# Attention with pooled queries and two MLPs: maxima tiles of every other query, and row maxima read back from memory with half the transfers

## The chip, the cores and the metric

The kernel runs on one core of one Trainium2 chip. The metric is the device time of one execution in microseconds (us), lower is better. In the trace the engines are PE (TensorE's matmuls), PEld (TensorE's weight loads, which overlap PE), DVE (VectorE), ACT (ScalarE), POOL (GpSimd) and SP (SyncE, which issues nearly all DMAs; SPq is its queue of instructions).

## What is computed

Queries are averaged in pairs, attention runs over 2 x 8 heads with 576 pooled queries and 1152 keys of width 64, and the result, as 1152 tokens of width 512, goes through two MLPs (mish, then ELU) of inner width 2048:

```python
q_pool = q.reshape(B, H, S // 2, 2, D).mean(axis=3)      # (2, 8, 576, 64)
scores = scale * np.matmul(q_pool, k.transpose(0, 1, 3, 2))
scores = scores - np.max(scores, axis=-1, keepdims=True)
attn = np.exp(scores)
attn = attn / (np.sum(attn, axis=-1, keepdims=True) + 1e-09)
x = np.matmul(attn, v)             # heads side by side: (1152, 512)
h = x @ w_in;  x = (h * np.tanh(softplus(h))) @ w_out    # first MLP
h = x @ w_in2; x = np.where(h > 0, h, np.exp(h) - 1) @ w_out2
```

## The kernel before

**Pairs of heads.** Attention works on 8 pairs of heads one after the other, head 0 on partitions 0 to 63 and head 1 on partitions 64 to 127. A pair takes 18 steps: 9 blocks of 128 keys (kt) for the first 256 queries (c = 0), then 9 for the other 320 (c = 1). In a step `qk` (L363) forms the transposed scores, keys on partitions and queries along the free axis, as a sum of four matmuls a head: three products of high and low parts of K and Q, and a fourth that adds a row, the negated maximum of each query's scores, with a matrix `unit` that copies row 0 (head 0) or row 64 (head 1) of the tile `tops` to all 128 keys. ACT then takes the exponent (L372). `av` (L443) multiplies with V.

**The maxima.** The row must be known before a pair's scores are exponentiated, so it is made while the pair before is worked on. `peak_mm` multiplies the high parts again, now with queries as weights, so that 128 queries lie on partitions and keys along the free axis: tiles 0 to 3 of 128 queries (L279 for the first 1024 keys, L286 for the last 128 keys of all four tiles), and the last 64 queries of both heads together (L293). DVE takes maxima of them (`peak`, L300, L302, L304) and `top` writes them, negated, to `neg`: one partition a query, one column a tile and head. So they lie down a column and must become a row. That is done through memory: `top_out` (L336) writes `neg` to `hopm` in DRAM, `top_in` (L342, L347) reads it back along the free axis of `tops`. Each pair from 1 on does this twice: a **first round** for tiles 0 and 1, whose row is needed at the pair's first step by the fourth matmuls (128x256), and a **second round** for tiles 2 and 3 and the last 64 queries, needed nine steps later (128x320). Pair 0 uses no memory for it: `flip` turns its maxima with matmuls, and ACT copies them to `tops` (L326).

**Order of the work.** Everything is in program order on each engine, written out by a table: `PREP` and `PLAN` give for each item the step at which its instructions are put on their queue (`top` is the step of `top_out` after the last maximum, and that of `top_in` after it). SP issues its DMAs strictly in that order, so that an issue that waits or takes long holds up those behind it: behind the first round's reads stand the sums' write (`sum_out`, L415) and the next pair's K (`load_k`, L226), ahead of them a part of the MLP weights (L109) and of V (L239). ACT's copy of the high part of K (`high_k`, L256) waits for that load in ACT's own order, with exponents behind it. After the pairs come the two MLPs, `h_mm` (L178) and `out_mm` (L736).

Of the kernel before, what the change touches and what calls it, by code (L numbers as in the profile page):

```python
# [11 lines left out]
F32 = mybir.dt.float32  # L12
F32R = mybir.dt.float32r
# [3 lines left out]
ALU = mybir.AluOpType  # L17
AX = mybir.AxisListType
# [4 lines left out]
def tile_pool_attention_mish_elu_mlp(  # L23
# [16 lines left out]
    nc = tc.nc  # L40
    B, H, S, D = v.shape
    NT, DM = out.shape
    DFF = moe_w_in.shape[1]
    P = 128
# [3 lines left out]
    NQ = SQ // P  # L48
# [18 lines left out]
    dp = ctx.enter_context(tc.tile_pool(name="hop", bufs=2, space=bass.MemoryType.DRAM))  # L67
# [115 lines left out]
    def attention():  # L183
        with ExitStack() as st:
            ap = st.enter_context(tc.tile_pool(name="attn", bufs=2))
# [3 lines left out]
            def take():  # L189
                i = 2 * next(ring)  # L190
                return banks[:, i:i + 2]

            half = [slice(0, D), slice(D, P)]
# [4 lines left out]
            def fixed(name, shape, dt, one=()):  # L198
                x = ap.tile(shape, dt, name=name, bufs=1)
                y = x.bitcast(F32) if dt is F32R else x  # L200
                nc.gpsimd.memset(y, 0.0)
                for r in one:
                    nc.gpsimd.memset(y[r:r + 1], 1.0)
                return x

            tops = [fixed(f"top{i}", [P, SQ], F32R) for i in range(2)]
            blks = [fixed(f"blk{i}", [P, P], F32R) for i in range(2)]
            unit = fixed("unit", [P, P], F32R, one=(0, D))
            pad = fixed("pad", [P, NQ + 1, 2, D], F32)
# [5 lines left out]
            raw_k, raw_q, kh, kl, qh, ql, vs = {}, {}, {}, {}, {}, {}, {}  # L215
            hops, tots, rbs, stat, neg, pts, adds, sc, sums_, acc, xs = {}, {}, {}, {}, {}, {}, {}, {}, {}, {}, {}
# [50 lines left out]
            def evs(n):  # L267
                return EVW if n else EVN

            def peak_mm(n, e):  # L270
                t, j = evs(n)[e]
                kw = 512 if n else KB
                if e == 0:
                    stat[n] = ap.tile([P, NQ + 1, 2, 3], F32, tag="stat", name="stat")
                    neg[n] = ap.tile([P, NQ + 1, 2], F32R, tag="neg", name="neg")
                pt = sc[n, e] = take()
                if t < NQ:
                    for h in range(2):
                        nc.tensor.matmul(  # L279
                            pt[:, h, :kw], qh[n][half[h], t * P:(t + 1) * P], kh[n][half[h], j * kw:(j + 1) * kw],  # L280
                            start=True, stop=True,
                        )
                elif t > NQ:
                    for x in range(NQ):
                        for h in range(2):
                            nc.tensor.matmul(  # L286
                                pt[:, h, x * P:(x + 1) * P], qh[n][half[h], x * P:(x + 1) * P], kh[n][half[h], S - P:],
                                start=True, stop=True,
                            )
                else:  # L290
                    side = banks[:, 6, 512 - P:]
                    for i, x in enumerate((pt[:, 0], pt[:, 1], side)):
                        nc.tensor.matmul(x, blks[n % 2], kh[n][:, 512 * i:min(512 * (i + 1), S)], start=True, stop=True)  # L293

            def peak(n, e):
                t, j = evs(n)[e]
                kw = 512 if n else KB
                pt, m = sc.pop((n, e)), stat[n]
                if t < NQ:
                    nc.vector.tensor_reduce(m[:, t, :, j], pt[:, :, :kw], axis=AX.X, op=ALU.max)  # L300
                elif t > NQ:
                    nc.vector.tensor_reduce(m[:, :NQ, :, 2].rearrange("p t h -> p h t"), pt.rearrange("p h (t k) -> p h t k", k=P), axis=AX.X, op=ALU.max)  # L302
                else:
                    nc.vector.tensor_reduce(m[:, t, 0, 0:2], pt, axis=AX.X, op=ALU.max)  # L304
                    nc.vector.tensor_reduce(m[:, t, 0, 2:3], banks[:, 6, 512 - P:], axis=AX.X, op=ALU.max)
                if e == (4 if n else 5):
                    top(n, 0, 2)
                elif e == len(evs(n)) - 1:
                    top(n, 2, NQ)

            def top(n, t0, t1):
                m, g = stat[n], neg[n] if n else pad[:, :, :, 0]
                nc.vector.tensor_reduce(g[:, t0:t1, :], m[:, t0:t1], axis=AX.X, op=ALU.max, negate=True)
                if t1 == NQ:
                    nc.vector.tensor_reduce(g[:, t1, 0:1], m[:, t1, 0:1], axis=AX.X, op=ALU.max, negate=True)


            def flip(t0, t1):
                pt = take()[:, 0]
                for t in range(t0, t1):  # L320
                    nc.tensor.matmul(
                        pt[:, (t - t0) * P:(t - t0 + 1) * P], pad[:, t].rearrange("p h r -> p (h r)"), ident,
                        start=True, stop=True,
                    )
                if t0 < NQ:
                    nc.scalar.copy(tops[0][:, t0 * P:t1 * P], pt[:, :(t1 - t0) * P])  # L326
                else:
                    for h in range(2):
                        nc.scalar.copy(tops[0][half[h], NQ * P:], pt[half[h], half[h]])

            def top_out(n, t0, t1):
                if t0 == 0:
                    hops[n] = dp.tile([P, NQ + 1, 2], F32, tag="hopm", name="hopm")
                e = slice(2 * t0, 2 * t1 + (t1 == NQ))
                hop, g = (x.rearrange("p t h -> p (t h)")[:, e] for x in (hops[n], neg[n]))
                nc.sync.dma_start(out=hop, in_=g.bitcast(F32))  # L336

            def top_in(n, t0, t1):
                hop, row = hops[n], tops[n % 2]
                for h in range(2):  # L340
                    r = h * D
                    nc.sync.dma_start(  # L342
                        out=row[r:r + 1, t0 * P:t1 * P].rearrange("o (t p) -> o t p", p=P).bitcast(F32),
                        in_=hop[:, t0:t1, h].rearrange("p t -> t p").unsqueeze(0),
                    )
                    if t1 == NQ:
                        nc.sync.dma_start(  # L347
                            out=row[r:r + 1, NQ * P:].bitcast(F32), in_=hop[half[h], NQ, 0:1].rearrange("p o -> o p")
                        )

# [174 lines left out]
            for n in range(n_pairs):  # L527
                s0 = n * NS
                if n:
                    prep = PREP[min(n, 2)]  # L530
                    for i in range(2):
                        at(s0 + prep["load_q"][i], "sp", load_q, n, slice(0, SQ), slice(i, i + 1))
                        at(s0 + prep["load_k"][i], "sp", load_k, n, kcut[i])
                        at(s0 + prep["load_v"][i], "sp", load_v, n, i)
                        at(s0 + prep["high_k"][i], "act", high_k, n, kcut[i])
                        at(s0 + prep["low_k"][i], *(("rest", low_k, n, nc.vector) if i == 0 else ("pool", low_k, n, nc.gpsimd)), kcut[i])
                    at(s0 + prep["pool_q"], "pool", pool_q, n, nc.gpsimd)
                    at(s0 + prep["high_q"], "act", high_q, n)
                    at(s0 + prep["blk_q"], "act", blk_q, n)
                    at(s0 + prep["low_q"], "pool", low_q, n, nc.gpsimd)  # L540
                    for e, r in enumerate(prep["peak"]):
                        at(s0 + r // 2, ("peak", "late")[r % 2], peak_mm, n, e)
                        at(s0 + r // 2, "dve", peak, n, e)
                    for (i, o), r, t0, t1 in zip(prep["top"], (prep["peak"][4], prep["peak"][-1]), (0, 2), (2, NQ)):
                        at(s0 + r // 2 + i, "sp", top_out, n, t0, t1)
                        at(s0 + r // 2 + i + o, "sp", top_in, n, t0, t1)
                plan = LAST if n == n_pairs - 1 else PLAN
                for c in range(2):
# [5 lines left out]
                    t0 = s0 + plan["total"][c]  # L554
# [39 lines left out]
            for e in (0, 3, 1, 4, 2, 5):  # L594
                peak_mm(0, e)
                peak(0, e)
            spots = [banks[:, 6:8]]
            qk(0, 0, 0, 1, spots[0], slice(3))
            for e in range(6, 8):
                peak_mm(0, e)  # L600
            flip(0, 2)
            for e in range(6, 8):
                peak(0, e)
# [15 lines left out]
            s = 0  # L619
            while s < last + 9:  # L620
                n, c, kt = s // NS, (s % NS) // KT, s % KT
# [5 lines left out]
                m = 2 if not c and kt in two else 0 if not c and kt - 1 in two or s < 1 else 1  # L627
# [215 lines left out]
    with tc.manual_schedule():  # L843
        attention()
        mlps()
# [36 lines left out]
```

## Time and profile before

| | |
|---|---|
| time, median of 3 runs | 634.15 us (634.05 to 636.31) |
| time of the profiled execution | 635.57 us |
| its span, first to last instruction | 633.8 us |
| PE busy | 616.9 us (97%) |
| DVE, ACT, POOL busy | 445.9, 335.1, 197.9 us (70%, 53%, 31%) |
| DMA packets | 50797, of which 17656 under 512 B |

The span is 1.8 us less than the time of the same execution. Attention takes about the first 228 us of it, the MLPs the rest. PE is the busiest engine by far, so time is to be had where it stands still, or where its own work gets shorter or longer.

### The profile page before, as it was taken

What the parts mean: (1) busy time and instruction counts of PE and PEld (TensorE: products, weight loads), DVE (VectorE), ACT (ScalarE), POOL (GpSimd) and SP (SyncE); (2) the same over time, 40 slices, a digit from 0 to 9 for tenths busy, and PEclk for the clock granted to TensorE, in tenths of its full rate; (3) what the DMA queues carried; (4) which work ended last, traced back from release to release, by engine and by line L of the source; (5) the groups of instructions that cost most, each with busy time, mean ns of one, the idle gap of its engine ahead of it and who ended that gap; (6) DMA issues with size and microseconds to landing.
All of it is one profiled execution on the core that took longest, in us unless ns stands there. A gap on an engine that the chain in (4) does not pass through costs nothing.

```text
span 633.8 us, 11509 instructions
## 1 busy us (share of the span) xinstructions
PE 616.9 (97%) x4498; PEld 535.2 (84%) x4498; DVE 445.9 (70%) x705; ACT 335.1 (53%) x675; POOL 197.9 (31%) x191
## 2 busy tenths in 40 slices
PE   5899999999999999999999999999999999999997
PEld 3667676676776689999999999999999999999995
DVE  5868767787787468647548657759878788995453
ACT  3665546555565544434344553456666657664441
POOL 5666565657653511101104323333210101100000
PEclk9999999999999999999999999999999999999999
DMA  4234252442523425223232222222232223300111
GB/s 140 84 99 123 67 134 60 131 111 66 132 64 89 89 76 176 67 67 104 68 97 82 85 71 97 97 70 62 72 99 68 66 68 100 109 25 11 40 51 50
DMA packets 50797, 53.34 MB, mean 84 GB/s; under 512 B 17656, under 2 KB 40248, under 8 KB 50744
## 3 DMA queue, kind: packets, MB, share of 16 engines
q1 hardware_dynamic: 50520, 52.29, 28.6%
q8 instruction: 35, 0.57, 0.4%
q10 hardware_dynamic: 224, 0.33, 0.2%
q14 instruction: 18, 0.15, 0.1%
HBM read 50.14 MB, written 2.47 MB: 83 GB/s over the span
## 4 chain that ended last, share of the span: by engine, by line
PE 86%; DMA 6%; DVE 3%; SPq 2%; issue 1%; ACT 1%; DVEq 0%; ACTq 0%
PE banks L178 32%; PE banks L736 31%; PE banks L363 10%; PE banks L443 8%; DMA top<-hopm 3%; PE banks L279 2%; PE banks L398 2%; DVE stat L300 1%; DMA hopm<-neg 1%; PE banks L293 1%; DVE stat L302 1%; DMA kr<-in_k_dram 1%; SPq L342 1%; DMA raw<-in_moe_w_in_dram 1%; DMA qr<-in_q_dram 1%
## 5 line engine op out<-in xcount | busy, mean ns | idle before, releaser
L178 PE MATMUL banks<-XH,wh 128*128 128x384 f32 x384 | 129.5, 337 | 0.0
L178 PE MATMUL banks<-XL,wh 128*128 128x384 f32 x384 | 129.4, 337 | 0.0
L178 PE MATMUL banks<-XH,wl 128*128 128x384 f32 x384 | 129.4, 337 | 0.0
L123 POOL TENSOR_SCALAR wf<-wf 128x512 f32<-128x512 f32 x64 | 43.6, 682 | 256.2 <-ACT wf L119 225.8
L372 ACT ACTIVATE pt<-banks 128x640 f32<-128x640 f32 (+2 forms) x136 | 88.0, 681 | 63.1 <-PE banks L363 62.7
L300 DVE TENSOR_REDUCE stat<-banks 128x2 f32<-128x1024 f32 (+1 forms) x68 | 77.9, 1171 | 13.2 <-PE banks L279 13.0
L443 PE MATMUL banks<-pt,vr 128*64 128x320 f32 (+1 forms) x576 | 79.6, 414 | 0.0
L178 PEld LDWEIGHTS banks<-XH,wh 128*128 128x128 f32 x384 | 72.0, 188 | 2.3 <-issue 0.5
L178 PEld LDWEIGHTS banks<-XL,wh 128*128 128x128 f32 x384 | 72.0, 188 | 1.8
L178 PEld LDWEIGHTS banks<-XH,wl 128*128 128x128 f32 x384 | 72.0, 188 | 0.0
L690 ACT ACTIVATE gh<-banks 128x384 fp32r<-128x384 f32 x48 | 23.7, 493 | 78.7 <-PE banks L178 78.7
L736 PE MATMUL banks<-gh,wl 128*128 128x384 f32 x192 | 64.5, 336 | 0.0
L736 PE MATMUL banks<-gl,wh 128*128 128x384 f32 x192 | 64.5, 336 | 0.0
L736 PE MATMUL banks<-gh,wh 128*128 128x384 f32 x192 | 64.4, 335 | 0.0
L443 PEld LDWEIGHTS banks<-pt,vr 128*64 128x64 f32 x576 | 37.9, 136 | 27.9 <-issue 5.5
L383 POOL TENSOR_TENSOR add<-pt 128x640 f32<-128x640 f32 (+1 forms) x30 | 43.0, 1434 | 52.4 <-ACT pt L372 52.3
L736 PE MATMUL banks<-wh,gl 128*128 128x512 f32 x144 | 56.2, 390 | 0.0
L736 PE MATMUL banks<-wl,gh 128*128 128x512 f32 x144 | 56.2, 390 | 0.0
L736 PE MATMUL banks<-wh,gh 128*128 128x512 f32 x144 | 56.2, 390 | 0.0
L693 DVE TENSOR_TENSOR gl<-g,gh 128x384 fp32r<-128x384 f32 x48 | 31.1, 649 | 34.1 <-ACT g L691 34.1
L383 POOL TENSOR_TENSOR add<-add,pt 128x640 f32<-128x640 f32 (+1 forms) x31 | 47.1, 1521 | 17.9 <-DVE add L383 11.7
L363 PE MATMUL banks<-QH,KH 64*128 64x320 f32 (+1 forms) x288 | 49.8, 332 | 1.2 <-DVE stat L300 0.6
(85 smaller groups left out, 1220.9 us busy)
## 6 DMA issues: line engine op xcount, KB each, us to landing
raw<-in_moe_w_in_dram SPq DMA_DIRECT2D x28, 512.0 KB
raw<-in_moe_w_out_dram SPq DMA_DIRECT2D x28, 512.0 KB
vr<-in_v_dram SPq DMA_DIRECT2D x16, 288.0 KB
qr<-in_q_dram SPq DMA_DIRECT2D x14, 288.0 KB
kr<-in_k_dram SPq DMA_DIRECT2D x7, 384.0 KB
raw<-in_moe_w_in_dram SPq DMA_DIRECT2D x8, 256.0 KB
raw<-in_moe_w_out_dram SPq DMA_DIRECT2D x8, 256.0 KB
out_dram<-part SPq DMA_DIRECT2D x8, 256.0 KB
```

What stands on the lines that cost most here:

```text
L123: nc.gpsimd.tensor_scalar(self.f, self.f, HUGE, -HUGE, op0=ALU.min, op1=ALU.max)
L178: nc.tensor.matmul(pt[:, :TB], w[:, kk * P:(kk + 1) * P], x[:, kk, tk], start=(i == 0), stop=(i == len(terms) - 1))
L279: nc.tensor.matmul(pt[:, h, :kw], qh[n][half[h], t * P:(t + 1) * P], kh[n][half[h], j * kw:(j + 1) * kw], start=True, stop=True,)
L300: nc.vector.tensor_reduce(m[:, t, :, j], pt[:, :, :kw], axis=AX.X, op=ALU.max)
L363: nc.tensor.matmul(pt[:, h, t * w:(t + 1) * w], x[half[h], k0:k0 + P] if x is not None else unit[half[h], :], y[half[h], cols], start=(i = ...
L372: nc.scalar.activation(pts[n, c][:, kt:kt + m], sc.pop((n, c, kt)), AF.Exp, scale=SCALE)
L383: eng.tensor_tensor(d, d if i is None else p[:, i], p[:, j], op=ALU.add)
L398: nc.tensor.matmul(pt[32 * g:32 * (g + 1), :w], ones[:, :32], x[:, h, z * w:(z + 1) * w], start=(i == 0), stop=(i == len(srcs) - 1), tile_ ...
L443: nc.tensor.matmul(acc[n, c][half[h], :w], vs[n][:, h, kt, :], pts[n, c][:, kt, h, :], start=(kt == 0), stop=(kt == KT - 1),)
L690: nc.scalar.activation(gh, h, AF.Mish)
L693: nc.vector.tensor_tensor(gl, g, gh, op=ALU.subtract)
L736: nc.tensor.matmul(pt, l, r, start=(first and i == 0), stop=(final and i == 2))
```

## The change

A tile of 128 queries was 128 neighbours; now tiles 0 and 1 share the first 256 queries, one takes the even and the other the odd ones, and tiles 2 and 3 share the next 256 in the same way. The weights that `peak_mm` loads are therefore every other column of `QH` (`rows`), in L279 and in L286. `neg` and `hopm` hold 9 columns in place of 10, ordered by head and then tile, so that the two tiles of a head lie side by side: the maxima of queries 2p and 2p + 1 are 8 neighbouring bytes of row p, and `top_in` reads both heads in one DMA, whose destination is rows 0 and 64 of `tops`. The first round has one read in place of two, the second round two in place of four. The tail of 64 queries is read for both heads in one DMA as well. In pair 0 ACT's copy (L326) puts the two tiles' columns between each other. The number of matmuls, weight loads and operations of DVE, ACT and POOL stays the same, and so does the table.

```diff
--- before.py
+++ after.py
@@ -267,24 +267,29 @@
             def evs(n):
                 return EVW if n else EVN
 
+
+            def rows(n, h, t):
+                x = qh[n][half[h], t // 2 * 2 * P:(t // 2 + 1) * 2 * P]
+                return x.rearrange("d (p t) -> d t p", t=2)[:, t % 2]
+
             def peak_mm(n, e):
                 t, j = evs(n)[e]
                 kw = 512 if n else KB
                 if e == 0:
                     stat[n] = ap.tile([P, NQ + 1, 2, 3], F32, tag="stat", name="stat")
-                    neg[n] = ap.tile([P, NQ + 1, 2], F32R, tag="neg", name="neg")
+                    neg[n] = ap.tile([P, 2 * NQ + 1], F32R, tag="neg", name="neg")
                 pt = sc[n, e] = take()
                 if t < NQ:
                     for h in range(2):
                         nc.tensor.matmul(
-                            pt[:, h, :kw], qh[n][half[h], t * P:(t + 1) * P], kh[n][half[h], j * kw:(j + 1) * kw],
+                            pt[:, h, :kw], rows(n, h, t), kh[n][half[h], j * kw:(j + 1) * kw],
                             start=True, stop=True,
                         )
                 elif t > NQ:
                     for x in range(NQ):
                         for h in range(2):
                             nc.tensor.matmul(
-                                pt[:, h, x * P:(x + 1) * P], qh[n][half[h], x * P:(x + 1) * P], kh[n][half[h], S - P:],
+                                pt[:, h, x * P:(x + 1) * P], rows(n, h, x), kh[n][half[h], S - P:],
                                 start=True, stop=True,
                             )
                 else:
@@ -309,10 +314,11 @@
                     top(n, 2, NQ)
 
             def top(n, t0, t1):
-                m, g = stat[n], neg[n] if n else pad[:, :, :, 0]
-                nc.vector.tensor_reduce(g[:, t0:t1, :], m[:, t0:t1], axis=AX.X, op=ALU.max, negate=True)
+                m = stat[n]
+                g = neg[n][:, 2 * t0:2 * t1].rearrange("p (h t) -> p t h", h=2) if n else pad[:, t0:t1, :, 0]
+                nc.vector.tensor_reduce(g, m[:, t0:t1], axis=AX.X, op=ALU.max, negate=True)
                 if t1 == NQ:
-                    nc.vector.tensor_reduce(g[:, t1, 0:1], m[:, t1, 0:1], axis=AX.X, op=ALU.max, negate=True)
+                    nc.vector.tensor_reduce(neg[n][:, 2 * NQ:] if n else pad[:, NQ, 0:1, 0], m[:, NQ, 0:1], axis=AX.X, op=ALU.max, negate=True)
 
 
             def flip(t0, t1):
@@ -323,30 +329,25 @@
                         start=True, stop=True,
                     )
                 if t0 < NQ:
-                    nc.scalar.copy(tops[0][:, t0 * P:t1 * P], pt[:, :(t1 - t0) * P])
+                    nc.scalar.copy(tops[0][:, t0 * P:t1 * P].rearrange("r (p t) -> r t p", t=2), pt[:, :2 * P].rearrange("r (t p) -> r t p", t=2))
                 else:
                     for h in range(2):
                         nc.scalar.copy(tops[0][half[h], NQ * P:], pt[half[h], half[h]])
 
             def top_out(n, t0, t1):
                 if t0 == 0:
-                    hops[n] = dp.tile([P, NQ + 1, 2], F32, tag="hopm", name="hopm")
+                    hops[n] = dp.tile([P, 2 * NQ + 1], F32, tag="hopm", name="hopm")
                 e = slice(2 * t0, 2 * t1 + (t1 == NQ))
-                hop, g = (x.rearrange("p t h -> p (t h)")[:, e] for x in (hops[n], neg[n]))
-                nc.sync.dma_start(out=hop, in_=g.bitcast(F32))
+                nc.sync.dma_start(out=hops[n][:, e], in_=neg[n][:, e].bitcast(F32))
 
             def top_in(n, t0, t1):
-                hop, row = hops[n], tops[n % 2]
-                for h in range(2):
-                    r = h * D
-                    nc.sync.dma_start(
-                        out=row[r:r + 1, t0 * P:t1 * P].rearrange("o (t p) -> o t p", p=P).bitcast(F32),
-                        in_=hop[:, t0:t1, h].rearrange("p t -> t p").unsqueeze(0),
-                    )
-                    if t1 == NQ:
-                        nc.sync.dma_start(
-                            out=row[r:r + 1, NQ * P:].bitcast(F32), in_=hop[half[h], NQ, 0:1].rearrange("p o -> o p")
-                        )
+                hop, row = hops[n], tops[n % 2].rearrange("(h d) s -> h d s", h=2)[:, 0].bitcast(F32)
+                nc.sync.dma_start(
+                    out=row[:, t0 * P:t1 * P].rearrange("h (p t) -> h p t", t=2),
+                    in_=hop[:, 2 * t0:2 * t1].rearrange("p (h t) -> h p t", h=2),
+                )
+                if t1 == NQ:
+                    nc.sync.dma_start(out=row[:, NQ * P:], in_=hop[:, 2 * NQ:].rearrange("(h j) o -> h (j o)", h=2))
```

**SP, the first round's read of one pair.** `top_85` is the row tile of every second pair, 1x256x1 the elements that one DMA writes, as rows by runs by elements of a run. Before:

```order
L239 DMA vr<-in_v_dram 128x576
L342 DMA top_85<-hopm 1x256x1 x2
L415 DMA hop<-sum 4x128
L226 DMA kr<-in_k_dram 128x768
L419 DMA tot<-hop 128x4
```

With the change, at the same place (lines are shifted by one to five):

```order
L239 DMA vr<-in_v_dram 128x576
L345 DMA top_85<-hopm 2x128x2
L416 DMA hop<-sum 4x128
L226 DMA kr<-in_k_dram 128x768
L420 DMA tot<-hop 128x4
```

One issue stands where two stood, and the sums' write and the load of K follow it directly.

**SP, the second round's reads of the same pair.** Before:

```order
L419 DMA tot<-hop 128x5
L342 DMA top_85<-hopm 1x256x1
L347 DMA top_85<-hopm 1x64x1
L342 DMA top_85<-hopm 1x256x1
L347 DMA top_85<-hopm 1x64x1
L427 DMA pop<-tot 128x5
L109 DMA raw<-in_moe_w_out_dram 128x512
```

With the change:

```order
L420 DMA tot<-hop 128x5
L345 DMA top_85<-hopm 2x128x2
L350 DMA top_85<-hopm 2x64x1
L428 DMA pop<-tot 128x5
L109 DMA raw<-in_moe_w_out_dram 128x512
```

Two issues stand where four stood; the last one is now the second from the first.

## Rows read from the trace of the kernel before

**Rows 1.** The page's part 4: the chain that ended last, by engine.

```profile
PE 86%; DMA 6%; DVE 3%; SPq 2%; issue 1%; ACT 1%; DVEq 0%; ACTq 0%
```

**Rows 2.** Windows: stretch, its length, busy us of each engine, clock, DMA share, GB/s.

```profile
54.39:81.58 27.19, 26.51 (x295) 18.92 (x293) 20.26 (x30) 15.08 (x30) 16.43 (x13) 1.00 0.42 109
81.58:109.13 27.55, 26.21 (x296) 18.37 (x293) 21.15 (x30) 15.21 (x30) 16.82 (x13) 1.00 0.38 95
109.13:134.85 25.72, 25.72 (x295) 18.17 (x293) 20.68 (x30) 15.09 (x30) 16.63 (x13) 1.00 0.42 105
134.85:161.27 26.42, 26.09 (x295) 18.37 (x293) 19.91 (x30) 15.09 (x30) 16.34 (x13) 1.00 0.41 97
161.27:188.00 26.73, 26.20 (x296) 18.47 (x293) 20.87 (x30) 15.10 (x30) 16.59 (x13) 1.00 0.40 103
...
232.00:634.00 402.00, 397.26 (x2139) 379.29 (x2137) 278.50 (x461) 208.16 (x433) 64.22 (x78) 1.00 0.24 76
```

**Rows 3.** Timeline of PE: start us, us, operation, at the first window's edge.

```profile
54.39 0.58 PE L286 MATMUL banks<-KH,QH 64*128 64x128 f32 x8
```

**Rows 4.** Waits of PE and PEld, 20 to 232: us in total, times, longest.

```profile
PE banks L363 <- DMA top<-hopm: 2.2, 4, 0.8
PE banks L279 <- ACT pt L372: 1.3, 1, 1.3
...
PEld banks L363 <- DMA top<-hopm: 3.7, 6, 1.0
```

**Rows 5.** Timeline of PEld: the longest wait for a read.

```profile
211.92 0.18 PEld L363 LDWEIGHTS banks<-top,unit 64*128 64x128 f32 x1 [1.02 <-DMA top<-hopm]
```

**Rows 6.** Timeline of SP, 138 to 158: one pair's two rounds.

```profile
138.93 3.86 SPq L342 DMA_DIRECT2D top<-hopm  x2
...
143.92 0.39 SPq L226 DMA_DIRECT2D kr<-in_k_dram  x1
...
154.13 0.66 SPq L342 DMA_DIRECT2D top<-hopm  x1
154.84 0.96 SPq L347 DMA_DIRECT2D top<-hopm  x1
155.85 0.63 SPq L342 DMA_DIRECT2D top<-hopm  x1
156.52 0.96 SPq L347 DMA_DIRECT2D top<-hopm  x1
```

**Rows 7.** The chain that ended last, in order of time: two landings of reads.

```profile
139.63 5.76 DMA top<-hopm
...
209.01 2.81 DMA top<-hopm
```

**Rows 8.** Timeline of PE: the two heads' first fourth matmuls of one pair.

```profile
171.23 0.28 PE L363 MATMUL banks<-top,unit 64*128 64x256 f32 x1
172.04 0.38 PE L363 MATMUL banks<-top,unit 64*128 64x256 f32 x1 [0.53 <-DMA top<-hopm]
```

**Rows 9.** Timeline of SP, 85 to 91.

```profile
85.73 3.37 SPq L342 DMA_DIRECT2D top<-hopm  x2
89.20 0.93 SPq L415 DMA_DIRECT2D hop<-sum  x1
90.23 0.38 SPq L226 DMA_DIRECT2D kr<-in_k_dram  x1
```

**Rows 10.** Timelines of ACT and of PE, 93 to 97.

```profile
95.16 0.83 ACT L256 CAST KH<-kr 128x768 fp32r<-128x768 f32 x1 [4.67 <-DMA kr<-in_k_dram]
...
93.37 1.83 PE L443 MATMUL banks<-pt,vr 128*64 128x320 f32 x12
96.54 0.50 PE L279 MATMUL banks<-KH,QH 64*128 64x512 f32 x2 [1.33 <-ACT pt L372]
```

**Rows 11.** The chain: one run of L286, eight loads and matmuls.

```profile
54.57 0.41 PE banks L286 x8
```

**Rows 12.** The DMA view, 155.4 to 158.4.

```profile
DMA packets 647, 0.00 MB, mean 1 GB/s; under 512 B 647, under 2 KB 647, under 8 KB 647
```

## The prediction

> **What bounds the kernel now.** I read the chain that ended last first: PE holds 86% of it and DMAs 6% [rows 1]. A chain names work, not loss, so the windows come next. I cut attention where each run of L286 begins, once a pair [rows 3], which gives five stretches of the same work [rows 2]. In the third PE is busy for all of its 25.72 us. The others take 26.42 to 27.55 us, and four of the five hold idle time of PE. The five sum to 133.61 us; five times 25.72 is 128.60, so 5.01 us are lost over five pairs. The MLPs' window shows 397.26 us of 402.00 busy, with the idle rest at the kernel's end; nothing of the change touches it but its start. So the question is what PE waits for in attention. Of what ends its waits there, the DMA `top<-hopm` is the largest that comes with every pair: 3.7 us on PEld in 6 waits (the longest 1.0), the same waits seen on PE as 2.2 us in 4; beside it one wait of 1.3 us for an exponent [rows 4]. The longest wait for a read stands in the last pair's second round [rows 5], outside the five windows.
>
> **What is removed, first round.** SP issues the two heads' reads one behind the other, 3.86 us for both [rows 6], 3.37 us in another pair [rows 9]. One issue of this shape alone takes 0.66 us [rows 6], so the second is held up for some 2.5 to 3 us behind what is already queued; its landing comes 5.76 us after its issue began [rows 7]. PE shows whose read was late: the first head's matmul started at 171.23 without a wait, the second's at 172.04 after one [rows 8]. So the first head's row was there by 171.23, 0.8 us ahead of the second's. The change reads both heads with the number of runs that one head had (256, of 8 bytes in place of 4), issued where the first read stood. If a run of 8 bytes costs what one of 4 does, it lands when the first head's did and this wait is gone. The other two waits of a first round are shorter and go with it.
>
> **Second round.** Four issues start at 154.13, 154.84, 155.85 and 156.52 [rows 6]. The last landing comes 2.81 us after the last issue's start [rows 7], in another pair. With two issues the last one starts 0.71 us after the first instead of 2.39, so that it lands 1.68 us earlier if its time to landing is the same. The longest wait there is 1.02 us [rows 5], so all three should go, with 0.6 us to spare.
>
> The Trainium skill (DMA: Bandwidth & Descriptors, "Rules for kernel authors") speaks against one part of this: an outermost dimension below 16 confines a DMA to as many engines, and the tail's read, one row of 64 before, now has an outermost dimension of two. By it the tail would be 64 runs on each of two engines, behind the 128 of the main read; no row here tells engines apart, so the trace neither agrees nor disagrees yet.
>
> The tail's 128 runs have a price in rows, should they stand in line behind the main read. The 640 elements of a whole second round pass as single packets in a window of 3 us [rows 12] (7 other packets lie in it), under 5 ns each, so 128 runs are 0.6 us at the most. That is about what there is to spare, so the forecast keeps the term at nothing.
>
> **What moves.** Behind the first round's reads SP issues the sums' write and the load of K. In the pair of [rows 9] K's load starts at 90.23, and ACT stands 4.67 us until it lands, with exponents queued behind; PE then waits 1.33 us for a bank that one of these exponents frees, from 95.20 (93.37 + 1.83) to 96.54 [rows 10]. Without the second issue, K's load starts 3.37 - 0.66 = 2.7 us earlier. If it lands that much earlier, at 92.4 in place of 95.1, ACT's copy (0.83) and exponent are over before PE asks at 95.20, and the 1.33 us go too. If the large loads ahead of it hold it back all the same, they stay: the term lies between 0 and 1.3 us. I take 1.3, since ACT needs only 1.3 of the 2.7 us.
>
> **What is added.** Nothing in count. Every other column is now read as weights in L279 and L286. No row shows a load at such a stride. From below, a load costs nothing more. From above I double it: L286's eight loads and matmuls take 0.41 us [rows 11], 51 ns each, about what 128 columns take at 2.4 GHz (53 ns; the granted clock is 1.00 in these windows [rows 2]). Two heads' matmuls work on different rows of the array and could run together, so I read this as the pace of the loads. Doubled, that is 0.41 us in each of 7 pairs, 2.9 us; and two loads of L279, 0.10 us, in each of 68 places (12 in pair 0, 8 in each other pair) if nothing hides them, 6.9 us. Together 9.8 us. I take nothing, since nothing in the rows says that a load's stride counts, and most of L279's loads have a matmul of 320 or 512 columns beside them.
>
> The Trainium skill (SBUF — State Buffer, "Door 1: The DMA port swizzle") says that SBUF gives full rate while two accesses fall into each line of 16 bytes, which two columns of 4 bytes at this stride do; by it the term is nothing as well. No run here shows it yet.
> ACT's copy in pair 0 and DVE's small reductions write the same elements at other places; I take nothing, and some 0.4 us once at the most.
>
> **The sum.** From below: 3.7 us of waits for reads and 1.3 us for the exponent [rows 4], 5.0 us. From above: the 5.01 us of the five windows [rows 2] and the last pair's 1.02 us [rows 5], 6.0 us. I take 5.6, between them. The profiled execution took 635.57 us and would take 630.0; that is 0.88% less. The median of the runs is 1.4 us below the profiled execution, so I carry the share over: 634.15 less 0.88% is 628.6 us.
>
> **The rivals.**
> (a) The reads get little faster: runs of 8 bytes are split to 4, or the one DMA takes as long as two. For it: two rows are written, and 512 elements are still moved. Against it: the window's packets stand in for runs, 640 for 640 elements [rows 12], so a longer run should make fewer. Then the second round still saves two issues, 1.7 us of SP, the first round keeps part of its waits and K's load comes no earlier: about 3.5 us, 630.6.
> (b) The waits move. PE gets rid of the reads and stands for the next thing, an exponent or a maximum that was just in time. For it: DVE is busy 20.87 of 26.73 us and PE has waited for exponents too. Against it: the window of 25.72 us has the same work on all engines and no idle PE at all [rows 2]. Then some 2.5 us are left: 631.6, within 0.5%.
> (c) The weight loads at a stride slow PE. 9.8 us at the most, less the 5.6: 638.4, slower. It decides from 5.6 / 9.8 on, when a load takes about 1.6 times as long and nothing hides it. For it: L286 runs at the pace of its loads [rows 11]. Against it: nothing but what was said above.
>
> **Chances.** The forecast 0.63, (a) 0.10, (b) 0.15, (c) 0.12. A measurement of this kernel can tell about 0.5%, 3.2 us, from no change. The forecast and most of (a) are faster by more: 0.70. (b), the rest of (a) and the mild end of (c) are the same: 0.20. The rest of (c) is slower: 0.10. The range reaches from 627.0, a little over 1 us past the sum's upper bound for what the windows don't cover (startup and the pair after it), to 633.0, past (a) and (b); (c) stays outside. The likeliest case alone is 627.5 to 630.
>
> **What would show it.** Right: waits of L363 for `top<-hopm` near zero; first rounds' issues one of 0.7 us; windows between runs of L286 all close to 25.7 us; fewer packets under 512 B by 3584 (28 reads of 256 and 14 of 64, 8064, become 14 of 256 and 7 of 128, 4480); no wait of 1.3 us in L279; mean weight load in L279 still as before. Wrong: a run of L286 above 0.45 us, or windows that are all longer by the same amount, would be (c); packets unchanged, (a); PE waiting for `pt`, `stat` or `rb` in places where it didn't, (b).

## The result and the profile after

The changed kernel takes 630.01 us (median of four runs, 629.94 to 630.47); the kernel before, run beside it on the same chip, 634.89 us (four runs, 634.05 to 636.31). The ratio is 0.9917, with a 95% interval of 0.9898 to 0.9936: 0.83% faster, where 0.88% was forecast; two later comparisons on other chips give 1.00% and 0.88% (runs 5 and 10). The profiled execution took 630.04 us with a span of 628.3 us, 5.5 us less span than before.

The five windows of attention between the runs of L291 (L286 before), which answer to [rows 2]; the columns are start and end, length, busy time of PE, PEld, DVE, ACT and POOL with the number of instructions, granted clock, DMA share and GB/s:

```profile
55.03:80.78 25.75, 25.75 (x295) 18.25 (x293) 21.03 (x30) 15.10 (x30) 16.59 (x13) 1.00 0.42 112
80.78:106.53 25.75, 25.75 (x296) 18.25 (x293) 20.85 (x30) 15.11 (x30) 16.59 (x13) 1.00 0.39 101
106.53:132.27 25.74, 25.74 (x295) 18.24 (x293) 20.70 (x30) 15.10 (x30) 16.60 (x13) 1.00 0.38 101
132.27:158.00 25.73, 25.73 (x295) 18.24 (x293) 20.02 (x30) 15.08 (x30) 16.02 (x13) 1.00 0.46 109
158.00:183.75 25.75, 25.75 (x296) 18.24 (x293) 21.01 (x30) 15.09 (x30) 16.60 (x13) 1.00 0.39 104
sum 128.72, PE 128.72 PEld 91.22 DVE 103.62 ACT 75.48 POOL 82.40; mean PE 25.74 PEld 18.24 DVE 20.72 ACT 15.10 POOL 16.48
```

PE is busy for the whole of each window. The sum is 128.72 us where it was 133.61: 4.89 us are gained here. All waits of PE from the start to 232 us (engine, line and tile that wait, what for; total, times, longest), against [rows 4]:

```profile
PE banks L284 <- ACT QH L246: 6.1, 1, 6.1
PE banks L284 <- DVE stat L305: 0.7, 2, 0.4
PE banks L364 <- DVE stat L305: 0.6, 2, 0.4
PE banks L364 <- ACT top L332: 0.5, 1, 0.5
PE banks L327 <- DVE pad L319: 0.5, 1, 0.5
PE banks L364 <- ACT pt L373: 0.2, 1, 0.2
PE banks L298 <- DVE stat L305: 0.2, 1, 0.2
```

No wait for a read of maxima is left, and none of 1.3 us for an exponent. What remains lies in the startup. The shares of the chain, against [rows 1], say the same of the whole span, PE 86% before and 96% now:

```profile
PE 96%; DVE 2%; DMA 1%; ACT 0%; issue 0%; SPq 0%; DVEq 0%
```

The first line of the waits is a loss that the forecast doesn't have. In the timeline of PE before (start, duration, instruction, and in brackets the idle time ahead of it with what ended it), the first maxima tile starts at 4.69, on ACT's copy of K:

```profile
4.69 0.69 PE L279 MATMUL banks<-KH,QH 64*128 64x384 f32 x2 [4.69 <-ACT KH L256]
6.00 1.42 PE L279 MATMUL banks<-KH,QH 64*128 64x384 f32 x6 [0.62 <-ACT QH L246]
```

After, it starts at 6.11, on a copy of Q. The same timeline of the changed kernel, and ACT's copy that it waits for:

```profile
6.11 1.33 PE L284 MATMUL banks<-KH,QH 64*128 64x384 f32 x6 [6.11 <-ACT QH L246]
...
5.75 0.30 ACT L246 CAST QH<-qr 128x128 fp32r<-128x128 f32 x1 [1.12 <-DVE qr L243]
```

Pair 0's Q comes in loads of 128 columns, and this is the second one's copy. A tile of the even queries of 256 needs both; a tile of 128 neighbours needed only the first. Only part of the 1.42 us comes through: pair 0's first run of L291 starts at 28.65 where L286's started at 27.66, 0.99 us later. The chain (start, us, what) says which part. Behind the first matmuls on the second load of Q stand DVE's reductions of the maxima, five of them before and six after:

```profile
6.73 4.42 DVE stat L300 x5
```

```profile
6.84 5.29 DVE stat L305 x6
```

Before, DVE took the first tile's maxima while the second load of Q was still on its way; now that reduction comes behind the load too and makes the chain 0.87 us longer. The remaining 0.11 is Q itself, whose copy lets PE start at 6.11 in place of 6.00.

With that the 5.5 us add up. From pair 0's run to pair 6's it is 160.34 us before (27.66 to 188.00) and 155.10 after (28.65 to 183.75), 5.24 less; what follows falls from 445.8 (633.8 - 188.00) to 444.55 (628.3 - 183.75), 1.25 less, the last pair's second round among it; and the startup costs 0.99.

SP's issues, against [rows 9] and [rows 6], both rounds:

```profile
85.31 0.54 SPq L345 DMA_DIRECT2D top<-hopm  x1
85.94 2.27 SPq L416 DMA_DIRECT2D hop<-sum  x1
88.31 0.39 SPq L226 DMA_DIRECT2D kr<-in_k_dram  x1
...
136.34 0.54 SPq L345 DMA_DIRECT2D top<-hopm  x1
136.98 3.05 SPq L416 DMA_DIRECT2D hop<-sum  x1
140.12 0.39 SPq L226 DMA_DIRECT2D kr<-in_k_dram  x1
...
150.83 0.56 SPq L345 DMA_DIRECT2D top<-hopm  x1
151.45 0.99 SPq L350 DMA_DIRECT2D top<-hopm  x1
```

The first round's read is issued in 0.54 us, but the hold has not gone: the sums' write behind it (L416) now stands 2.27 and 3.05 us, where L415 took 0.9. So K's load gains less. Counted from the start of its pair's run, it went from 8.65 us (90.23 - 81.58) to 7.53 (88.31 - 80.78) in one pair and from 9.07 (143.92 - 134.85) to 7.85 (140.12 - 132.27) in another. ACT's wait for K in the pair of [rows 10]:

```profile
91.64 0.83 ACT L256 CAST KH<-kr 128x768 fp32r<-128x768 f32 x1 [1.95 <-DMA kr<-in_k_dram]
```

1.95 us in place of 4.67, which was enough for PE to wait for no exponent here. Over all pairs ACT's waits for K fell from 18.7 us in 6 to 9.7 in 6.

The weight loads (PEld's groups by line, operation and tile: busy us and mean ns of one, then idle time and what ended it), before and after:

```profile
L279 PEld LDWEIGHTS banks<-KH,QH 64*128 64x128 f32 x110 | 10.2, 184 | 9.4 <-ACT pt L372 4.3 <-ACT wh L142 2.9 <-issue 1.2
```

```profile
L284 PEld LDWEIGHTS banks<-KH,QH 64*128 64x128 f32 x112 | 10.9, 192 | 8.2 <-ACT wh L142 3.0 <-issue 2.4 <-ACT pt L373 2.4
```

A load of every other column takes 192 ns, one of neighbours 184. DMA packets, against [rows 12]'s kind, over the whole run:

```profile
DMA packets 46976, 53.35 MB, mean 85 GB/s; under 512 B 13834, under 2 KB 36426, under 8 KB 46922
```

Before there were 17656 under 512 B, so 3822 are gone; 3584 were forecast. The forecast counted runs alone, and the number of DMAs counts too: run 2, with 21 reads more than the changed kernel and runs as long, has 14464, 630 more. The longer runs by themselves thus took 3192 away and the merging 630.

### The profile page after: what moved, and what is told of

Read it like the earlier page. It is cut to its first block, busy times and chain, and to the rows that moved or that the text cites. A ratio compares the mean times of both kernels' runs of the same rounds, so it can differ in the third digit from the quotient of the medians.

```text
span 628.3 us, 11496 instructions
## 1 busy us (share of the span) xinstructions
PE 614.9 (98%) x4498; PEld 534.9 (85%) x4498; DVE 448.0 (71%) x705; ACT 335.4 (53%) x675; POOL 197.5 (31%) x191
## 4 chain that ended last, share of the span: by engine, by line
PE 96%; DVE 2%; DMA 1%; ACT 0%; issue 0%; SPq 0%; DVEq 0%
PE banks L178 32%; PE banks L737 31%; PE banks L364 14%; PE banks L444 12%; PE banks L284 3%; PE banks L399 2%; DVE stat L305 1%; PE banks L298 1%; DMA qr<-in_q_dram 1%; PE banks L291 0%; DVE part L762 0%; PE banks L327 0%; ACT pt L373 0%; SPq L233 0%; ACT top L332 0%
## 5 line engine op out<-in xcount | busy, mean ns | idle before, releaser
L717 ACT CAST gh<-g 128x384 fp32r<-128x384 f32 x48 | 24.7, 514 | 48.2 <-DVE g L711 47.9
```

Source lines behind the costliest of these rows:

```text
L717: nc.scalar.copy(gh, g)
```

## The experiments

The theory after the result: both heads' reads in one DMA take the waits away, the hold behind the first read moves to the sums' write, the stride of the weights costs next to nothing, and pair 0's tiles cost 1 us at the start. The rivals: it is the 8-byte runs that help and not the number of DMAs; it is the place in SP's order, of V ahead of the reads (run 3) or of K behind them (run 6); the stride costs, hidden in windows that gained more than they show.

### 1. Pair 0 in neighbours

```diff
             def rows(n, h, t):
+                if n == 0:
+                    return qh[n][half[h], t * P:(t + 1) * P]
...
-                    nc.scalar.copy(tops[0][:, t0 * P:t1 * P].rearrange("r (p t) -> r t p", t=2), pt[:, :2 * P].rearrange("r (t p) -> r t p", t=2))
+                    nc.scalar.copy(tops[0][:, t0 * P:t1 * P], pt[:, :2 * P])
```

> The changed kernel, but pair 0 keeps tiles of neighbouring queries (it turns its maxima with matmuls and needs no read). Theory: in the changed kernel the first matmul starts 1.4 us later (6.1 in place of 4.7 us) because the even queries of the first 256 need both loads of Q, and pair 0 ends 1.0 us later for it; then this kernel starts at 4.7 us and takes 629.0 us. Rival: the later start is chance, or ACT's strided copy of the maxima (388 ns in place of 370); then the time stays at 630.0 us.

629.24 us against 635.85 for the kernel before, 0.9898 (0.9885 to 0.9912), span 627.5. PE's waits of its first 10 us:

```profile
PE banks L286 <- ACT KH L256: 4.7, 1, 4.7
PE banks L286 <- ACT QH L246: 0.6, 1, 0.6
PE banks L286 <- DVE stat L307: 0.4, 1, 0.4
```

PE starts at 4.7 us again, five reductions stand in the chain again (4.43 us), and pair 0's run stands at 27.72, where before had it at 27.66. The cause of the startup loss is shown. Its size in the end time needs the two kernels on one chip (run 9).

### 2. The heads apart again, in runs of 8 bytes

```diff
+                for g in ((0, 1), (1, 2)):
+                    g = slice(*g)
-                    out=row[:, t0 * P:t1 * P].rearrange("h (p t) -> h p t", t=2),
-                    in_=hop[:, 2 * t0:2 * t1].rearrange("p (h t) -> h p t", h=2),
+                        out=row[g, t0 * P:t1 * P].rearrange("h (p t) -> h p t", t=2),
+                        in_=hop[:, 2 * t0:2 * t1].rearrange("p (h t) -> h p t", h=2)[g],
```

The tail is split in the same way, so there are six DMAs in a pair.

> The changed kernel with one read a head again (six DMAs in a pair), each still in runs of 8 bytes. Theory that the number of reads counts (the second issue of a round is held up, and the last one starts late): the second round again starts its last issue 2.4 us after its first, waits of the fourth matmuls for the reads come back to 2 us or more, windows between the runs of 128-column maxima matmuls are 26 us and more, 632 to 634 us. Rival that the length of a run counts: packets halve all the same, the waits stay away, windows of 25.75 us, 630 us.

632.02 us, 0.9942 (0.9927 to 0.9957), span 630.2: 0.58% faster than before, and 2.0 us slower than the changed kernel's 630.01. Of PE's waits for reads 0.6 us in two are left, where 2 us or more were expected. SP's first round in one pair:

```profile
60.49 1.16 SPq L347 DMA_DIRECT2D top<-hopm  x2
61.75 0.53 SPq L416 DMA_DIRECT2D hop<-sum  x1
62.37 0.39 SPq L226 DMA_DIRECT2D kr<-in_k_dram  x1
```

Two reads of one row, 128 runs each, go out in 1.16 us, and the sums' write behind them takes 0.53; it is 0.53 to 0.59 us in all seven pairs (in one of them the two reads take 2.66). So neither theory holds alone: halving the number of runs takes away most of the waits and of the hold, and merging the heads brings 2.0 us more. The waits for reads account for 0.6 of these at the most; against the changed kernel the five windows are 0.67 us longer (129.39), the stretch behind the last run 0.77 (445.32). One read for both heads in runs of 4 bytes was not tried.

### 3. The kernel before, with V's load after the reads

```diff
-                "load_v": [-1, 9],
+                "load_v": [0, 9],
...
-                "load_v": [-3, 0],
+                "load_v": [-2, 0],
```

(`PREP[1]` and `PREP[2]` of the table, in the kernel before.)

> The kernel before with one edit: the first load of V for the next pair stands behind the first round's reads and the sums' write in SP's order, no longer ahead of them. Theory that a first round's read is late because of the large loads ahead of it in the queue: the second issue of the first round falls from 2 to 3 us to about 1 us, the three waits of the first rounds (1.6 us on the weight loads) go, the second rounds' stay; 632 to 633 us. Rival that the reads' own 512 runs of 4 bytes take the time: the waits stay as they are, 634 to 635 us.

635.13 us, 0.9988 (0.9978 to 0.9997), span 632.5. The first rounds' waits are gone, and PEld's waits for reads fall from 3.7 us in 6 to what the second rounds hold:

```profile
PEld banks L363 <- DMA top<-hopm: 1.7, 3, 0.9
```

SP's hold gets shorter but stays with V's load out of the way. The pair of [rows 6]:

```profile
138.25 3.27 SPq L342 DMA_DIRECT2D top<-hopm  x2
141.62 0.95 SPq L415 DMA_DIRECT2D hop<-sum  x1
```

This is the longest of the seven: the two reads take 1.70 to 3.27 us, where they took 2.54 to 3.86 before, and each pair's is shorter than it was. The windows sum to 131.36 us, 2.25 less than before's, but the startup is 0.9 us longer in this execution, and the median hardly moves: 632 to 633 us was expected. Moving V's load takes the same waits of the first round as the change does, not those of the second. V's load makes the hold on SP's second read longer, but about half of it is there without that load: both reads take 3.1 us in the mean before and 2.3 here, and two that are not held some 1.3.

### 4. Weights in neighbours everywhere

```diff
-                x = qh[n][half[h], t // 2 * 2 * P:(t // 2 + 1) * 2 * P]
-                return x.rearrange("d (p t) -> d t p", t=2)[:, t % 2]
+                return qh[n][half[h], t * P:(t + 1) * P]
```

> The changed kernel with neighbouring queries as weights in all pairs and the reads as changed, so that from pair 1 on each query gets the negated maximum of another query; the work is the same but for the stride. Theory that the stride costs next to nothing: the mean weight load of the maxima matmuls falls from 192 to 184 ns, windows stay at 25.7 us, and beside the kernel with only pair 0 in neighbours the time differs by less than 0.3 us, 629 us. Rival that a strided load costs 8 ns on PE's path each: 168 loads, 1.3 us less, 627.7 us.

629.28 us, 0.99 (0.9882 to 0.9917). A load takes 185 ns again, and the sum of the five windows is

```profile
sum 128.48, PE 128.48 PEld 90.75 DVE 102.00 ACT 75.49 POOL 82.51; mean PE 25.70 PEld 18.15 DVE 20.40 ACT 15.10 POOL 16.50
```

against 128.72: the stride costs 0.05 us a pair, some 0.3 us in all. The theory holds. The rest of the 0.73 us to the changed kernel (630.01, on another chip) is put down to the startup, where this kernel too begins at 4.7 us; it was not measured apart.

### 5. The changed kernel again

> The changed kernel itself, unedited, for comparison with the three below on one chip: 630.0 us by every theory.

630.14 us against 636.46, 0.9900 (0.9881 to 0.9919). The changed kernel's own time is the same as in the first comparison, 630.01; the ratio moves by 0.0017 because the kernel before varies more: its medians are 634.89, 635.85, 636.46 and 635.49 in the four comparisons.

### 6 and 7. One round apart

Run 2's loop in the first round alone, then in the second alone:

```diff
+                for g in ((0, 1), (1, 2)) if t0 == 0 else ((0, 2),):
```

```diff
+                for g in ((0, 1), (1, 2)) if t0 else ((0, 2),):
```

> The changed kernel with one read a head in the first round alone, in runs of 8 bytes. With all rounds apart no first round waited, so by the theory that the second round's last issue is what merging is worth, this takes 630.0 us, and the sums' write behind the reads is issued in 0.5 us in place of 2 to 3. Rival that merging is worth as much in each round: 631 us, with waits of the 128x256 fourth matmuls.

> The changed kernel with one read a head in the second round alone, in runs of 8 bytes. By the theory that the second round's last issue is what merging is worth: 631.5 to 632 us, with waits of the 128x320 fourth matmuls for the reads, as with both rounds apart. Rival that merging is worth as much in each round: 631 us.

First round apart: 630.89 us, 0.991 (0.9889 to 0.993), 0.75 above run 5. The time is nearer to the rival's 631 than to the theory's 630.0, but the waits that the rival named don't come: its windows are 25.75 and no read is waited for. The sums' write is issued in 0.55 to 0.59 us, as the theory had it. K's load then starts 6.0 us after its pair's run (87.47 - 81.45) in place of 7.53, and ACT's waits for K fall to 4.2 us, but the windows stay: an earlier K is worth nothing more here. The last pair holds a new wait, in PE's timeline:

```profile
209.99 0.43 PE L399 MATMUL banks<-add,ones 128*32 128x128 f32 x8 [0.64 <-POOL add L384]
```

POOL's sum stands behind DVE, which waits for the sums' read:

```profile
206.41 0.19 DVE L424 RECIPROCAL tot<-tot 128x5 f32<-128x5 f32 x1 [1.31 <-DMA tot<-hop]
```

Behind its last run of L291 this execution takes 445.47 us, 0.95 more than run 5's (444.52). Why that read lands later was not found.

Second round apart: 632.11 us, 0.9931 (0.9911 to 0.9951). The theory's time is met within about 0.1 us, but the reads' own wait is small, and a second one, for V, is new:

```profile
107.10 0.38 PE L364 MATMUL banks<-top,unit 64*128 64x320 f32 x1 [0.30 <-DMA top<-hopm]
...
59.45 1.94 PE L444 MATMUL banks<-pt,vr 128*64 128x256 f32 x14 [0.51 <-DMA vr<-in_v_dram]
```

The stretch with V's wait loses 1.2 us. Merging the second round is thus worth about 2 us (632.11 against 630.14), and of it the waits for reads that appear are only 0.3 us. The profiled executions of runs 6 and 7 took longest of their six (631.73 and 633.09 us), so each of these waits is seen once, and not in the execution that gave the median.

### 8. A stride of four columns

```diff
-                x = qh[n][half[h], t // 2 * 2 * P:(t // 2 + 1) * 2 * P]
-                return x.rearrange("d (p t) -> d t p", t=2)[:, t % 2]
+                x = qh[n][half[h], :NQ * P]
+                return x.rearrange("d (p t) -> d t p", t=NQ)[:, t]
```

> The changed kernel with every fourth of 512 queries as weights, in all pairs, so that maxima go to other queries than their own; the work is the same but for the stride, 16 bytes in place of 8. Theory that a load slows where less than two of its elements share 16 bytes: the mean weight load of the maxima matmuls rises well above 192 ns (to 250 or more), the run of eight 128-column matmuls above 0.5 us, windows to 26.5 us, 635 us. Rival that the stride does not count at this length either: loads of 192 to 200 ns, windows of 25.8 us, 630 us.

642.32 us, 1.0091 (1.0068 to 1.0115): slower than the kernel before. PEld's two groups and the sum of the five windows:

```profile
L284 PEld LDWEIGHTS banks<-KH,QH 64*128 64x128 f32 x114 | 17.6, 307 | 8.4 <-issue 3.7 <-ACT wh L142 2.9 <-ACT pt L373 1.2
...
L291 PEld LDWEIGHTS banks<-KH,QH 64*128 64x128 f32 x56 | 7.1, 322 | 0.0
```

```profile
sum 135.33, PE 135.33 PEld 97.83 DVE 103.67 ACT 75.53 POOL 82.83; mean PE 27.07 PEld 19.57 DVE 20.73 ACT 15.11 POOL 16.57
```

Columns 16 bytes apart cost 307 and 322 ns a load, and 1.33 us a pair (27.07 against 25.74). This is rival (c) at a stride where it holds, past the 1.6 from which it was to decide (307 / 184 is 1.7), and PE stays busy through all of it: a slower load shows as longer windows, not as waits. The first matmul waits until 9.0 us here, since its tile needs four loads of Q, and pair 0's run starts at 32.39 in place of 28.65. This and the size of the loss per pair put the time 7 us above the 635 that the theory gave.

### 9 to 11. The kernel of run 1 beside the changed one, and with the first round apart

Run 9 is run 1's kernel, run 10 the changed kernel, both on one chip; run 11 is run 9 with run 6's edit.

> The changed kernel with pair 0 in neighbouring queries, once more, now beside the changed kernel on one chip: by the theory of the later first matmul 0.8 to 1.0 us less than the changed kernel in the same call; if the earlier difference was between chips or runs, the same time.

> The changed kernel itself, unedited, beside the other two of this call: 630.1 us by every theory.

> Pair 0 in neighbouring queries and one read a head in the first round, runs of 8 bytes. If the first round gains nothing from merging: as the kernel with only pair 0 in neighbours, within 0.3 us. If merging counts there too: 0.7 us more than that.

Run 9: 629.03 us, 0.9901 (0.9888 to 0.9915). Run 10: 629.84 us, 0.9912 (0.9898 to 0.9925). Run 11: 630.13 us, 0.9917 (0.9903 to 0.9931). The medians put pair 0 in neighbours 0.8 us ahead of the changed kernel, the fastest version here. The intervals of the two ratios overlap, but four of run 9's five executions took less than each of run 10's five. The time of pair 0's run can't size this loss: in run 9's profiled execution, its longest (630.06 us), it stands at 28.42, later than run 10's 28.18, since PE keeps the pace of the start until 21.5 there and only until 17.7 in run 10 (last section). The reductions in the chain tell the kernels apart in every trace: five, 4.42 or 4.43 us, in the kernel before and in runs 1, 3, 4, 9 and 11, six, 5.29 us, in all others. Splitting the first round gives back 1.1 us, so merging counts there too, as run 6 had it with 0.75. Of that the traces show 0.52 us behind the last run of 128-column maxima matmuls (445.05 against 444.53), 0.26 of it a wait of the last pair's sums; the rest is not seen.

## Why the prediction was right, step by step

- **First round: right.** The waits are gone in all pairs. "It lands when the first head's did" was not measured by itself; that no matmul waits for the read is what the trace shows. What merging adds to the longer runs in this round, 0.75 and 1.1 us by runs 6 and 11, comes without any wait for a read, and the forecast has no term for it.
- **K's load: mis-sized, its effect right.** It was to start 2.7 us earlier and started 1.1 and 1.2 us earlier. The step took the hold for one that only a second read suffers; in all seven pairs it now falls on the sums' write, which is issued next. The 1.3 us exponent wait went all the same, since ACT's wait for K shrank from 4.67 to 1.95. Counted from the run, ACT's copy of K starts 2.7 us earlier (95.16 - 81.58 before, 91.64 - 80.78 after): the landing moved as far as forecast, though the issue moved by less than half of that. The load itself took 3.3 us from the start of its issue to its landing (88.31 to 91.64) where it took 4.9 (90.23 to 95.16); why was not tried. By the prediction's own count ACT needed 1.3 us, more than the issue moved, so that the exponent's wait went hangs on a quicker landing that the forecast didn't have: luck.
- **Second round: right.** The last issue starts 0.62 us after the first (150.83 to 151.45), for 0.71 forecast, and no wait is left. Run 7 gives the saving about 2 us when undone, part of it by way of V's load, which the forecast didn't have.
- **The tail at nothing: right.** Nothing waits for it. The Trainium skill (DMA: Bandwidth & Descriptors, "Rules for kernel authors") says that an outermost dimension below 16 confines a DMA to as many engines at most; no row here tells engines apart, so no run shows it. What the rows show is that the sums' write is held 2.27 and 3.05 us behind one read of two rows with 256 runs, and not behind two reads of one row with 128 each (run 2).
- **Strided loads at nothing: right to 0.3 us.** 192 ns against 184, 0.05 us a pair by run 4; the run of L291 takes 0.41 us in the chain as before. The upper bound of 9.8 us was no idle fear, and too low: it was for loads twice as long, and at four columns, with loads 1.7 times as long, the loss is 1.33 us a pair, 9.3 in seven, where the bound's share of it would be under 7. The Trainium skill (SBUF — State Buffer, "Door 1: The DMA port swizzle") promises full rate while two accesses fall into each line of 16 bytes. Columns 8 bytes apart do, and cost almost nothing; of those 16 bytes apart one falls into each line, and the load takes 1.7 times as long (307 ns against 184). On both the runs agree with the rule, though none shows that the lines are the cause. The same passage puts the free stride at four fp32; run 8 differs from that, and the measurement decides.
- **The startup: missed.** ACT's copy in pair 0 was costed at nothing and L332 is indeed 383 to 392 ns where L326 took 367 to 372; but the forecast looked only at that copy and not at what a tile of every other query waits for. This is the 0.99 us: one reduction of DVE, 0.87, that now waits for the second load, and 0.11 by which that load came later. Run 9 beside run 10 puts the loss at 0.8 us.
- **The sum.** Forecast 5.6 us, measured 5.5 of span: 4.89 in the windows (5.01 were lost there before), 0.35 in the stretch from pair 0's run to pair 1's (5.24 - 4.89), 1.25 behind the last run, less 0.99 at the start. Without the startup the gain is 6.5 us, 0.5 above the forecast's upper end of 6.0. So two misses cancel in part, and that the sum came so close is luck: outside the windows 1.6 us were gained (0.35 + 1.25) where the sum allowed 1.02, and the startup took about as much back as it lay above the 5.6. The median, 630.01, is 1.4 us above the 628.6 of the forecast, which carried the share over to a median of 634.15; the kernel before had 634.89 beside it.
- **The rivals.** (a) is out by the packets and by the issues. (b) didn't come: the windows close to 25.74 with PE busy throughout. (c) is out at a stride of two columns and true at four.

## What to carry to other kernels

When data is laid out in a new order so that a DMA reads longer runs, ask what the first tile now needs: a tile that takes every other column of a block needs the whole block, and at the start, with loads arriving piece by piece, that costs time; exempting the first pair gave back about 0.8 us. A strided weight load at two 4-byte columns was nearly free and at four was not, so measure the one stride that is used. When an issue on SP takes long, ask whether the DMA ahead of it is the cause: here, removing the held read moved the hold to the sums' write, its neighbour.

## What was not expected of the hardware

- **A hold on SP that changes with the shape of the DMA ahead, but not by it alone.** In the first rounds, with 256 runs of 4 bytes in one row the second read is held (2.54 to 3.86 us for both, 0.66 for one alone); with 256 runs of 8 bytes in two rows the sums' write is held in every pair, 1.45 to 3.05 us; behind two DMAs of 128 runs in one row each it is held in none, though once the second of them is (2.66 us for both, run 2). The same reads stand in the second rounds, and there no issue takes longer than 0.96 us before and 1.20 after. Just ahead of the first round stand large loads (in the pair of [rows 6] of Q, MLP weights and V), and without V's the hold is shorter (run 3). What decides is not shown.
- **TensorE's pace at the start.** At some 18.7 us the changed kernel's pairs of 256-column matmuls (one a head) still start 0.21 us apart, where later they start 0.12 us apart, though the granted clock of the stretch reads 1.00:

```profile
18.71 0.41 PE L364 MATMUL banks<-QH,KH 64*128 64x256 f32 x2
18.93 0.41 PE L364 MATMUL banks<-QH,KL 64*128 64x256 f32 x2
...
20.98 0.31 PE L364 MATMUL banks<-QH,KH 64*128 64x256 f32 x2
21.10 0.31 PE L364 MATMUL banks<-QH,KL 64*128 64x256 f32 x2
```

512 columns in 0.12 us would be over 4 GHz, so the two heads' matmuls run together. Then 256 columns in 0.21 us are 1.2 GHz, the lower of the clock's two levels (1.2 and 2.4 GHz), and in 0.12 us 2.1, which only the upper one allows. In the kernel before the same matmuls are 0.12 us apart from 17.52 on; in run 6 they are still 0.21 apart at 21.59. The step falls at different times in kernels whose startup is the same, so a difference of some tenths of a us between two profiled startups need not be an effect of an edit. The 0.99 us of the startup is none of this: the first matmuls of L364 start 0.97 us after those of L363 (10.07 against 9.10), before the step of either.
